# Attention and a two-layer FFN on one core: the 64 left-over keys of heads 8 to 19 join the softmax denominators on GpSimd instead of on TensorE

## The chip, the cores and the metric

The kernel runs on one core of a Trainium2 chip. The metric is the device time in microseconds (us) of one execution, as the median over several. TensorE (PE in the rows; PEld is its weight load), VectorE (DVE), ScalarE (ACT), GpSimd (POOL) and SyncE (SP) each work through a queue of their own in a fixed order; an instruction that has to wait holds up whatever stands behind it in its queue.

## The reference

Four sequences of 448 tokens, 12 heads of 64. Scores are capped by a tanh, softmax runs over the keys, and the heads' outputs, joined to rows of 768, pass through a layer norm without bias, two products with a ReLU between, and a residual:

```python
scores = cap * tanh((q @ k.T) / sqrt(64) / cap)
attn = exp(scores - max(scores)); attn = attn / (sum(attn) + 1e-9)
x = (attn @ v), heads joined                        # (4, 448, 768)
xn = (x - mean) / sqrt(var + 1e-6) * g_ln
out = x + relu(xn @ w_ch1) @ w_ch2                  # 768 -> 3072 -> 768
```

## The kernel before

Scores are kept with the keys on the partitions. 448 keys are three blocks of 128 and a rest of 64. Heads are worked on in quads (`quad`, line 499): four heads are two pairs, `p` = 0 and 1. For a pair, `products` (L707) makes the scores on TensorE (L724), ScalarE takes tanh (L769) and exp (L777) into a tile `es[p]` of 128 x (2 heads, 3 blocks, 448 queries); three such tiles exist at that stage. The rests of all four heads share one tile `er`: pair 0 on partitions 0 to 63, pair 1 on 64 to 127, each with its two heads side by side, 2 x 448 columns. Their scores are L750, their exp is L785.

Two things are made of the exponentials. The products with V go into two PSUM banks, by blocks (`pv`, L553) and then the rests (`pv_rest`, L560); they are copied out by L610 or L612. The denominators are sums over the keys: VectorE adds the three blocks of a pair into `s1` (L576, L578), two tiles of 128 x 896, of which two exist. Then `sums` (L630) multiplies `s1` with a column of ones on TensorE, one head to each 32 partitions of one PSUM bank: line L637, 4 products that show as 8 matmul records. What of the rests has to be added is done in one of two ways. For heads below `RESTS` = 20 the tile `er` is a second operand of `sums`: line L641, another 4 products with ones that are zero for the other pair's partitions. From head 20 on VectorE adds each half of `er` onto the same half of its pair's `s1` (L588, 64 x 896, one for each pair), and L641 is left out.

`finish` (L648) copies the sums to SBUF (`ss`; VectorE for heads 0 to 7, ScalarE from head 8), turns them on TensorE (L663) so that tokens lie on the partitions, adds epsilon and takes reciprocals on VectorE (L666, L669). The outputs are turned by four groups of two transposes (L677), each into a PSUM bank, and VectorE multiplies them by the reciprocals into the token tiles (L687). The padding of the turned tiles is zeroed on GpSimd (L620). After heads 8 to 11, the last of sequence 0, `norm` (L879) normalizes the first three token tiles: statistics (L859, L861), a power on GpSimd (L873), the subtraction and scaling on VectorE (L892), transposes (L900), and a split into two fp32r parts (L905 on ScalarE, L909 on VectorE). The first FFN products (L1020 to L1022) read these. FFN products then run in between the rest of the attention, up to 420 us; later stages are FFN alone (L1238 to L1241, L1331 to L1333).

GpSimd also unpacks the first four weight blocks (L949, L952, and their rounding in `round`, L493), which VectorE finishes (L955, L957, L496). The kernel's GpSimd DMAs (L1348) begin at 528 us.

No order is written out by hand. `add` (L158) records each operation with its engine, a cost, a due time, and the tiles it reads and writes. `emit` (L207) then plays the whole program through with those costs: each engine, when free, takes the operation of the earliest due time that is ready and whose buffers are to be had. The sequence that comes out is what each engine's queue gets. The waits on the chip come from the tiles that an instruction truly touches, not from `reads`. `LEAD` = 24 heads are due before the FFN's first products. The key `G` is GpSimd, `V` VectorE, `A` ScalarE, `T` TensorE.

Of the kernel before, what the change touches and what calls it, by code (L numbers as in the profile page):

```python
# [18 lines left out]
B, H, S, D = 4, 12, 448, 64  # L19
# [14 lines left out]
LEAD = 24  # L34
# [21 lines left out]
VEC2 = lambda n: 50 + 1.1 * n  # L56
# [28 lines left out]
GROUP = 4  # L85

FINE = 28
RESTS = 20
FIRST = 24


# [13 lines left out]
    e=('e', 3), e2=('e', 2), kh=('k', 2), kl=('k', 2), ot=('b', 4), ss=('b', 1), stage=('a', 3),  # L105
# [9 lines left out]
    e=('e', 2), t=('e', 2), ot=('b', 3), ss=('b', 1), stage=('a', 1),  # L115
# [32 lines left out]
class Order:  # L148
# [9 lines left out]
    def add(self, engines, fn, reads=(), writes=(), allocs=(), due=0.0, dma=0, after=(), lag=0.0):  # L158
        op = Op()
        (op.engine, op.cost), = engines.items()  # L160
        op.fn, op.due, op.dma, op.lag, op.seq = fn, due, dma, lag, len(self.ops)
        deps = set(after)
        for k in reads:
            deps.update(self.writer.get(k, ()))
        for k in writes:
            deps.update(self.writer.get(k, ()))
            deps.update(self.readers.get(k, ()))
        for k in writes:
            self.writer[k], self.readers[k] = [op], []
        for k in reads:  # L170
            self.readers.setdefault(k, []).append(op)
        deps.discard(op)
        op.left, op.outs, op.ready, op.end, op.wait, op.after = len(deps), [], 0.0, None, None, deps
        for d in deps:
            d.outs.append(op)
        bufs = {k[0] if isinstance(k, tuple) else k: 0 for k in (*reads, *writes, *allocs)}
        op.bufs = [b for b in bufs if isinstance(b, Buf)]
        for b in op.bufs:
            self.wide += b.wide and not b.users
            b.users += 1  # L180
            op.ready = max(op.ready, b.since)
        self.ops.append(op)
        return op
# [197 lines left out]
class Program:  # L381
# [25 lines left out]
    def buf(self, pool, tag, shape, dtype, bufs=1):  # L407
        size = 1
        for x in shape[1:]:
            size *= x  # L410
        kinds, tags = (GENERAL_KINDS, GENERAL_TAGS) if self.general else (KINDS, TAGS)
        if tag in tags:
            kind, n = tags[tag]
            self.limits[pool, tag] = n
            bufs, size = kinds[kind]
        else:
            kind = tag
        self.places[pool, kind] = bufs
        b = Buf(pool, kind, tag, shape, dtype)
        self.sizes[pool, kind] = max(size, self.sizes.get((pool, kind), 0))  # L420
        return b
# [77 lines left out]
    def quad(self, i, at):  # L499
# [3 lines left out]
        nc, add, buf = self.nc, self.add, self.buf  # L503
# [4 lines left out]
        for p in range(2):  # L508
            kq = self.given.get(i // 2 + p)
            if kq is None:  # L510
                kq = buf("att", "kq", [128, 2, S], F32)
                for k in range(2):
                    rows = slice(k * D, k * D + D)
                    add({"S": 550}, lambda e, h=i + 2 * p + k, rows=rows, kq=kq: nc.sync.dma_start(
                        out=kq.ap[rows], in_=self.kq[h, rows].rearrange("p (a s) -> p a s", a=2)),
                        writes=[(kq, k)], due=at(i + 2 * p) - PLAN["early"], dma=D * 2 * S * 4)
# [3 lines left out]
        for p in range(2):  # L520
            v = buf("att", "v", [128, 2, NJ, DV], F32)
            src = self.v[i + 2 * p:i + 2 * p + 2].rearrange("h p (j d) -> p h j d", d=DV)
            for a in range(2):
# [3 lines left out]
                    writes=[(v, a)], due=at(i + 2 * p) - PLAN["early"], dma=2 * KC * NJ * DV * 4)  # L527
# [8 lines left out]
        if split:  # L536
            parts.clear()
            for p, kq in enumerate(kqs):
                h, l = (buf("kr", t, [128, 2, S], F32R) for t in ("kh", "kl"))
                keys = [(kq, k) for k in range(2)]  # L540
                due = dues[p] - PLAN["qk"] - PLAN["ks"]
                add({"A": ACTS(2 * S)}, lambda e, h=h, kq=kq: self.round(e, h.ap, kq.ap), reads=keys, writes=[h], due=due)
                add({"V": VEC2(2 * S)}, lambda e, h=h, l=l, kq=kq: self.rest(e, l.ap, kq.ap, h.ap),
                    reads=[*keys, h], writes=[l], due=due)
# [20 lines left out]
        fine = i < FINE  # L565
# [6 lines left out]
        for p, e1 in enumerate(es):  # L572
            due = dues[p] - rush
            s1 = buf("att", "s1", [128, 2, S], F32)
            rows = slice(p * REST, p * REST + REST)
# [3 lines left out]
                out=s1.ap, in0=s1.ap, in1=e1.ap[:, :, 2], op=ALU.add), reads=[(e1, 0), (e1, 1)], writes=[s1], due=due)  # L579
            s1s.append(s1)  # L580

        if i < (FINE if self.general else RESTS):
            rests = [er]
        else:
            rests = []
            for p, s1 in enumerate(s1s):
                rows = slice(p * REST, p * REST + REST)
                add({"V": VEC2(2 * S)}, lambda e, s1=s1, rows=rows: nc.vector.tensor_tensor(  # L588
                    out=s1.ap[rows], in0=s1.ap[rows], in1=er.ap[rows], op=ALU.add), reads=[er], writes=[s1], due=dues[2] - rush)
        if merged:  # L590
            ps = self.sums(s1s, rests, dues[2] - rush, cost + F4(S), lambda: (pv(1), pv_rest()), [*v_all, *done(1), er], pos)
        else:
            for p in range(2):
                for blocks in [[j] for j in range(NK)] if i + p == 0 and not self.general else [range(NK)]:
                    add({"T": 200 + len(blocks) * F4(S)}, lambda e, p=p, blocks=blocks: pv(p, blocks),
                        reads=[*v_all, *(done(p) if len(blocks) > 1 else [(es[p], "e", j) for j in blocks])], writes=[pos[p]],
# [51 lines left out]
    def finish(self, i, pairs, ps, due, late):  # L648


        nc, add, buf = self.nc, self.add, self.buf
        b, h0 = divmod(i, H)
        part = HEADS[-(i < FRONT)]
        due += PLAN["fin"] if h0 + GROUP < H else 0
        ss, d0 = self.out_tile("ss", i, late)
        add({part["ss"]: dict(A=ACTP(S), V=VEC2(S))[part["ss"]]}, lambda e: self.copy(
            e, ss.ap[:, d0:d0 + S], ps.ap[:, :S]), reads=[ps], writes=[(ss, 0)], due=due)
        pr = buf("ps", "f", [128, 512], F32)
        r = buf("small", "r", [128, NK + 1, GROUP], F32, 2)

        def turn(e):
            for j in range(NK + 1):
                nc.tensor.transpose(pr.ap[:, j * 128:j * 128 + 128], ss.ap[:, j * 128:j * 128 + 128], self.ident)  # L663

        add({"T": 440}, turn, reads=[(ss, 0), (ss, 2)], writes=[pr], due=due)
        add({"V": 210}, lambda e: nc.vector.tensor_scalar(  # L666
            r.ap, pr.ap.rearrange("p (j c x) -> p j c x", j=NK + 1, c=GROUP)[:, :, :, 0], self.eps, None,
            op0=ALU.add), reads=[pr], writes=[r], due=due)
        add({"V": 220}, lambda e: nc.vector.reciprocal(r.ap, r.ap), writes=[r], due=due)  # L669
        W = GROUP * D  # L670
        cols = slice(h0 * D, h0 * D + W)
        for j, tl, p in self.token_tiles(b):
            pf = buf("ps", "f", [128, 512], F32)

            def turn(e, j=j, pf=pf):
                for c, ot in enumerate(pairs):
                    nc.tensor.transpose(pf.ap[:, c * 128:c * 128 + 128], ot.ap[:, j * 128:j * 128 + 128], self.ident)  # L677

            add({"T": len(pairs) * 110}, turn, reads=[(o, x) for o in pairs for x in (0, 2)] + [r] * self.general, writes=[pf], due=due)
            m = p.stop - p.start  # L680
            rows = lambda ap: ap.rearrange("p (h d) -> p h d", d=D)
            if tl < NA:
                writes, dst = [(self.home(tl)[0], tl, h0)], lambda tl=tl, p=p: self.x(tl)[p, cols]
            else:
                st = buf("att", "stage", [128, W], F32)
                writes, dst = [st], lambda st=st, p=p: st.ap[p]
            add({"V": VEC2(W)}, lambda e, j=j, p=p, m=m, dst=dst, pf=pf: nc.vector.tensor_tensor(  # L687
                out=rows(dst()), in0=rows(pf.ap[p, :W]), in1=r.ap[p, j].unsqueeze(2).to_broadcast([m, GROUP, D]),
                op=ALU.mult), reads=[pf, r], writes=writes, due=due)
            if tl >= NA:  # L690
                add({"V": 330}, lambda e, dst=dst, tl=tl, p=p: nc.vector.bn_stats(
                    self.stats.ap[p, tl % SLOTS, h0 // GROUP], dst()), reads=writes,
                    writes=[(self.stats, tl % SLOTS, h0 // GROUP, p.start)], due=due)
                add({"S": 550}, lambda e, dst=dst, tl=tl, p=p: nc.sync.dma_start(out=self.xd[tl][p, cols], in_=dst()),
                    reads=writes, writes=[("xd", tl, (h0, p.start))], due=due, dma=128 * W * 4)
# [883 lines left out]
```

## Time and profile before

| | us |
|---|---|
| median of 3 runs | 859.35 (858.87 to 860.08) |
| the profiled execution | 858.48 |
| its span, first to last instruction | 856.7 |
| mean granted TensorE clock | 0.999 |
| DMA traffic over the span | 148.96 MB, 174 GB/s |

The profile is of one execution. A share of busy time is an average over stages with different limits, so the rows below are read by stretch. A wait is put down to what released it. A matmul's duration is modelled, and neighbours overlap; what a group of matmuls costs is read from the start of the group to the start of the next.

### The profile page before, as it was taken

The page shows a single profiled execution, that of the slowest core. Times are in us where ns is not written, and L with a number is a line of the kernel's source. Part 1 is how long each engine was busy: PE and PEld are TensorE (multiplying, and loading weights), DVE is VectorE, ACT ScalarE, POOL GpSimd, SP SyncE. Part 2 cuts the span into 40 slices and gives each one's busy share as a digit, 9 for nine tenths or more (in the row PEclk, how much of TensorE's full clock was granted, in tenths as well). Part 3 has the DMA queues.
Part 4 walks back from the last instruction along what each step waited for, and adds up shares of the span by engine and source line. Part 5 has one row for each costly group of instructions (what it writes and reads, how often), then busy time and mean ns, then how long its engine had stood idle before and what let it go on. Part 6 is the DMA issues. An engine that isn't in the chain of part 4 may idle for free.

```text
span 856.7 us, 12856 instructions
## 1 busy us (share of the span) xinstructions
PE 845.3 (99%) x4700; PEld 705.2 (82%) x4700; DVE 702.6 (82%) x1157; ACT 512.1 (60%) x795; POOL 151.5 (18%) x198
## 2 busy tenths in 40 slices
PE   8999999999999999999999999999999999999997
PEld 4434477979879799799799989898988998999887
DVE  2689798878789788687689878888888888788896
ACT  7887777544653647354426646756575666566650
POOL 0233231101112111111110001223113211312210
PEclk9999999999999999999999999999999999999999
DMA  9696666565675774653673344897878888787984
GB/s 233 149 245 212 187 179 181 180 219 162 175 223 159 221 210 165 189 170 120 176 258 102 102 141 84 164 183 152 168 160 153 166 171 157 143 187 158 184 216 152
DMA packets 55579, 148.96 MB, mean 174 GB/s; under 512 B 7378, under 2 KB 20178, under 8 KB 55506
## 3 DMA queue, kind: packets, MB, share of 16 engines
q1 hardware_dynamic: 42256, 113.43, 44.9%
q0 software_dynamic: 12096, 33.04, 22.9%
q10 hardware_dynamic: 1154, 1.57, 0.5%
q8 instruction: 39, 0.64, 0.3%
q14 instruction: 34, 0.28, 0.1%
HBM read 87.46 MB, written 60.56 MB: 173 GB/s over the span
## 4 chain that ended last, share of the span: by engine, by line
PE 94%; ACT 2%; DVE 1%; issue 0%; POOL 0%; DVEq 0%; ACTq 0%
PE two L1238 7%; PE two L1241 7%; PE two L1239 7%; PE two L1331 7%; PE two L1333 7%; PE two L1332 7%; PE two L1020 6%; PE two L1049 6%; PE two L1022 6%; PE two L1021 6%; PE two L1051 6%; PE two L1050 6%; PE two L553 6%; PE two L724 5%; PE two L677 1%; PE two L637 1%
## 5 line engine op out<-in xcount | busy, mean ns | idle before, releaser
L1348 POOL DMA_DIRECT2D out_dram<-x x84 | 73.4, 1000 | 314.4 <-ACT x L1339 215.1
L1339 ACT ACTIVATE x<-two 128x384 f32<-128x384 f32 x168 | 79.6, 487 | 36.9 <-PE two L1333 26.2
L1020 PE MATMUL two<-hA,q 128*128 128x384 f32 x288 | 100.5, 349 | 0.0
L1238 PE MATMUL two<-X,q 128*128 128x512 f32 x252 | 99.2, 394 | 1.2 <-ACT y L1255 1.2
L1241 PE MATMUL two<-X,q 128*128 128x512 f32 x252 | 99.2, 394 | 0.0
L1239 PE MATMUL two<-X,q 128*128 128x512 f32 x252 | 99.0, 393 | 0.0
L1343 DVE TENSOR_TENSOR x<-two,x 128x384 f32<-128x384 f32 x144 | 77.0, 553 | 26.7 <-PE two L1333 22.8
L1049 PE MATMUL two<-w,hh 128*128 128x384 f32 x288 | 98.5, 342 | 0.0
L1022 PE MATMUL two<-hA,q 128*128 128x384 f32 x288 | 97.5, 339 | 0.0
L1021 PE MATMUL two<-lA,q 128*128 128x384 f32 x288 | 97.5, 338 | 0.0
L1051 PE MATMUL two<-w,hl 128*128 128x384 f32 x288 | 97.3, 338 | 0.0
L1050 PE MATMUL two<-w,hh 128*128 128x384 f32 x288 | 97.3, 338 | 0.0
L952 POOL TENSOR_SCALAR raw<-raw 128x768 f32<-128x768 f32 x48 | 48.7, 1017 | 229.4 <-ACT c L948 203.1
L1331 PE MATMUL two<-w,hop 128*128 128x384 f32 x264 | 89.0, 337 | 0.0
L1333 PE MATMUL two<-w,hop 128*128 128x384 f32 x264 | 88.8, 336 | 0.0
L1332 PE MATMUL two<-w,hop 128*128 128x384 f32 x264 | 88.8, 336 | 0.0
L1054 DVE TENSOR_TENSOR x<-two,x 128x384 f32<-128x384 f32 x144 | 76.0, 548 | 12.3 <-PE two L1051 11.8
L769 ACT ACTIVATE e<-two,sc 128x448 f32<-128x448 f32 (+1 forms) x108 | 75.0, 759 | 17.8 <-PE two L724 17.3
L489 ACT ACTIVATE w<-c 128x768 fp32r<-128x768 f32 x38 | 32.1, 846 | 60.6 <-DVE c L957 23.7
L1020 PEld LDWEIGHTS two<-hA,q 128*128 128x128 f32 x288 | 54.0, 188 | 10.9 <-issue 8.5
L777 ACT ACTIVATE e<-e,capt 128x1344 f32<-128x1344 f32 (+1 forms) x35 | 61.1, 1772 | 0.3
L553 PE MATMUL two<-e,v 128*64 128x448 f32 x288 | 59.2, 547 | 1.8 <-ACT e L769 0.9
(179 smaller groups left out, 1850.4 us busy)
## 6 DMA issues: line engine op xcount, KB each, us to landing
raw<-in_w_dram SPq DMA_DIRECT2D x48, 768.0 KB, 4.9
out_dram<-x POOLq DMA_DIRECT2D x84, 384.0 KB, 7.5
kept<-c SPq DMA_DIRECT2D x47, 384.0 KB, 5.5
d<-in_kq_dram SPq DMA_DIRECT2D x48, 224.0 KB, 5.6
d<-kept SPq DMA_DIRECT2D x23, 384.0 KB, 3.3
c<-kept SPq DMA_DIRECT2D x23, 384.0 KB, 7.9
v<-in_v_dram SPq DMA_DIRECT2D x24, 227.5 KB, 5.1
x<-out_dram SPq DMA_DIRECT2D x13, 384.0 KB, 5.4
```

What stands on the lines that cost most here:

```text
L1020: nc.tensor.matmul(ps.ap[:, :n], lhsT=w1h.ap[:, wc], rhs=xh.ap[:, c], start=(c == 0), stop=False)
L1021: nc.tensor.matmul(ps.ap[:, :n], lhsT=w1h.ap[:, wc], rhs=xl.ap[:, c], start=False, stop=False)
L1022: nc.tensor.matmul(ps.ap[:, :n], lhsT=w1l.ap[:, wc], rhs=xh.ap[:, c], start=False, stop=(c == CC - 1))
L1049: nc.tensor.matmul(o, lhsT=h[0].ap[:, mc], rhs=w[0].ap[:, hc], start=(f == 0), stop=False)
L1050: nc.tensor.matmul(o, lhsT=h[0].ap[:, mc], rhs=w[1].ap[:, hc], start=False, stop=False)
L1051: nc.tensor.matmul(o, lhsT=h[1].ap[:, mc], rhs=w[0].ap[:, hc], start=False, stop=(f == last))
L1238: nc.tensor.matmul(ps.ap, lhsT=wh.ap[:, wc], rhs=xs[c].ap[:, 0], start=start and c == 0, **o)
L1239: nc.tensor.matmul(ps.ap, lhsT=wh.ap[:, wc], rhs=xs[c].ap[:, 1], start=False, **o)
L1241: nc.tensor.matmul(ps.ap, lhsT=wl.ap[:, wc], rhs=xs[c].ap[:, 0], start=False, **o)
L1331: nc.tensor.matmul(o, lhsT=hh.ap[:, mc], rhs=wh.ap, start=begin, stop=False, **skip)
L1332: nc.tensor.matmul(o, lhsT=hh.ap[:, mc], rhs=wl.ap, start=False, stop=False, **skip)
L1333: nc.tensor.matmul(o, lhsT=hl.ap[:, mc], rhs=wh.ap, start=False, stop=True, **skip)
```

## The change

The number `RESTS` = 20 becomes a string with one letter for each of the first five quads: `T` for heads 0 to 7 (as before, L641), `G` for heads 8 to 19, and `V` (as before, L588) from head 20 on. For `G` the two additions of 64 x 896 that L588 does on VectorE are issued on GpSimd, and the planner counts 3000 ns for each; `sums` then has L637 alone. The additions read `er` and one `s1` each, and write that `s1`.

The second edit is in `finish`: for heads below `LEAD` = 24 the outputs' transposes (L677) name the copied sums `ss` among their reads. As they don't touch that tile, this holds for the planner's sequence and adds no semaphore.

```diff
--- before.py
+++ after.py
@@ -85,7 +85,7 @@
 GROUP = 4
 
 FINE = 28
-RESTS = 20
+RESTS = "TTGGG"
 FIRST = 24
 
 
@@ -579,13 +579,14 @@
                 out=s1.ap, in0=s1.ap, in1=e1.ap[:, :, 2], op=ALU.add), reads=[(e1, 0), (e1, 1)], writes=[s1], due=due)
             s1s.append(s1)
 
-        if i < (FINE if self.general else RESTS):
+        aside = RESTS[i // GROUP] if i < GROUP * len(RESTS) else "V"
+        if fine if self.general else aside == "T":
             rests = [er]
         else:
             rests = []
             for p, s1 in enumerate(s1s):
                 rows = slice(p * REST, p * REST + REST)
-                add({"V": VEC2(2 * S)}, lambda e, s1=s1, rows=rows: nc.vector.tensor_tensor(
+                add({"G": 3000} if aside == "G" else {"V": VEC2(2 * S)}, lambda e, s1=s1, rows=rows: self.eng(e).tensor_tensor(
                     out=s1.ap[rows], in0=s1.ap[rows], in1=er.ap[rows], op=ALU.add), reads=[er], writes=[s1], due=dues[2] - rush)
         if merged:
             ps = self.sums(s1s, rests, dues[2] - rush, cost + F4(S), lambda: (pv(1), pv_rest()), [*v_all, *done(1), er], pos)
@@ -676,7 +677,7 @@
                 for c, ot in enumerate(pairs):
                     nc.tensor.transpose(pf.ap[:, c * 128:c * 128 + 128], ot.ap[:, j * 128:j * 128 + 128], self.ident)
 
-            add({"T": len(pairs) * 110}, turn, reads=[(o, x) for o in pairs for x in (0, 2)] + [r] * self.general, writes=[pf], due=due)
+            add({"T": len(pairs) * 110}, turn, reads=[(o, x) for o in pairs for x in (0, 2)] + ([r] if self.general else [(ss, 0)] if i < LEAD else []), writes=[pf], due=due)
             m = p.stop - p.start
             rows = lambda ap: ap.rearrange("p (h d) -> p h d", d=D)
             if tl < NA:
```

## Rows read from the trace of the kernel before

**Rows 1.** The page: span; then busy us (share of the span) and instructions of each engine.

```profile
span 856.7 us, 12856 instructions
...
PE 845.3 (99%) x4700; PEld 705.2 (82%) x4700; DVE 702.6 (82%) x1157; ACT 512.1 (60%) x795; POOL 151.5 (18%) x198
```

**Rows 2.** Stretches: from:to, length, busy us (instructions) by engine, PE clock, DMA share, GB/s.

```profile
18.00:50.00 32.00, 31.89 (x196) 12.49 (x196) 24.07 (x38) 27.43 (x24) 6.18 (x11) 1.00 0.75 200
50.00:76.00 26.00, 25.04 (x149) 10.12 (x148) 21.34 (x37) 24.44 (x27) 12.24 (x13) 1.00 0.77 209
76.00:420.00 344.00, 344.00 (x2055) 281.40 (x2053) 284.35 (x436) 200.85 (x280) 54.67 (x72) 1.00 0.63 185
420.00:840.00 420.00, 418.82 (x2177) 382.28 (x2176) 358.68 (x617) 246.90 (x455) 76.93 (x87) 1.00 0.72 159
```

**Rows 3.** Waits of TensorE: waiter, releaser, us in total, times, longest.

```profile
PE two L900 <- DVE lA L909: 0.8, 1, 0.8
```

**Rows 4.** Chain of waits, 48 to 92 us: start us, us, what.

```profile
64.69 1.58 POOL mv L873
...
67.97 1.85 DVE xn L892 x3
...
74.78 1.07 PE two L900 x6
```

**Rows 5.** TensorE in order of time: start us, us, line, out<-in, count.

```profile
87.61 0.96 PE L637 MATMUL two<-d,ones 128*32 128x448 f32 x8
...
89.25 0.98 PE L560 MATMUL two<-d,v 64*64 64x448 f32 x8
...
105.12 0.96 PE L637 MATMUL two<-d,ones 128*32 128x448 f32 x8
106.01 0.98 PE L560 MATMUL two<-d,v 64*64 64x448 f32 x8
```

**Rows 6.** All matmuls of line L641: count, ns min/median/max, first and last start.

```profile
L641 PE MATMUL two<-d,ones x40: 539/539/539, 22.2 to 88.8; 128*32 128x448 f32 x40
```

**Rows 7.** ScalarE and VectorE in order of time: last inputs of the sums, heads 8 to 15.

```profile
46.33 1.04 ACT L785 ACTIVATE d<-d,capt 128x896 f32<-128x896 f32 x1
...
47.64 1.06 DVE L578 TENSOR_TENSOR d<-d,e 128x896 f32<-128x896 f32 x1
...
64.27 1.03 ACT L785 ACTIVATE d<-d,capt 128x896 f32<-128x896 f32 x1
...
66.97 1.08 DVE L578 TENSOR_TENSOR d<-d,e 128x896 f32<-128x896 f32 x1
```

**Rows 8.** GpSimd in order of time: start us, us, line, out<-in [idle before].

```profile
30.36 1.79 POOL L952 TENSOR_SCALAR raw<-raw 128x768 f32<-128x768 f32 x2
...
51.19 0.83 POOL L493 TENSOR_SCALAR q<-c 128x768 fp32r<-128x768 f32 x1 [5.43 <-DVE c L957]
...
101.05 1.63 POOL L952 TENSOR_SCALAR raw<-raw 128x768 f32<-128x768 f32 x1
```

**Rows 9.** VectorE in order of time: beside the first of rows 8, and after heads 16 to 19.

```profile
30.54 2.56 DVE L576 TENSOR_TENSOR d<-e 128x896 f32<-128x896 f32 x1 [0.17 <-ACT e L777]
...
91.48 1.09 DVE L576 TENSOR_TENSOR d<-e 128x896 f32<-128x896 f32 x1 [3.65 <-ACT e L777]
```

**Rows 10.** In order of time: TensorE and a ScalarE copy, heads 8 to 11; first FFN product.

```profile
50.17 0.96 PE L637 MATMUL two<-d,ones 128*32 128x448 f32 x8
...
52.76 0.66 PE L663 MATMUL two<-ident,b 128*128 128x128 f32 x4
...
56.36 0.96 ACT L610 ACTIVATE b<-two 128x448 f32<-128x448 f32 x2
...
57.89 1.09 PE L677 MATMUL two<-ident,b 128*128 128x128 f32 x8
...
84.65 0.44 PE L1020 MATMUL two<-hA,q 128*128 128x384 f32 x1
```

**Rows 11.** L576 over the whole run: count, ns min/median/max, first and last start.

```profile
L576 DVE TENSOR_TENSOR d<-e x24: 1029/1086/2555, 11.1 to 393.8; 128x896 f32<-128x896 f32 x24
```

## The prediction

> **What bounds the kernel now.** I began with the page's busy times: TensorE is busy 99% of the span, VectorE 82%, ScalarE 60%, GpSimd 18% [rows 1]. A busy matmul row is modelled, so I next took the stretches, to see where TensorE has any idle time that a rearranged queue could give back or add to. Between 18 and 50 us it lacks 0.11 us, between 50 and 76 us 0.96, between 76 and 420 us nothing, between 420 and 840 us 1.18 [rows 2]. So from 18 us on the span is a sum of TensorE's work with some 2.3 us of gaps in it, at the full granted clock, and work taken from TensorE should come off the end, unless a gap opens. Third, the list of TensorE's waits, for the largest gap near the change: 0.8 us, one wait of the layer norm's transposes L900 for VectorE's L909 [rows 3]. Fourth, the chain of waits around the edited quads. Between 52.9 and 74.8 us it does not run through TensorE for long: it goes over GpSimd's power L873, three subtractions L892 on VectorE, and ends at L900 [rows 4]. That is the one place before the FFN where VectorE and GpSimd decide when TensorE goes on, and the additions of heads 12 to 15 fall into it.
>
> **The products removed.** Duration alone misleads here, since the four 128x32 products of a group overlap: each record shows 539 ns [rows 6], which times eight would be 4.3 us. From start to start, heads 16 to 19 take 87.61 to 89.25 for L637 and L641 together, 1.64 us; heads 20 to 23, which have no L641, take 105.12 to 106.01, 0.89 us [rows 5]. The difference is 0.75 us. Of the 40 records 24 belong to the three quads (8 each) [rows 6], so TensorE loses 3 x 0.75 = 2.25 us of work. All three lie where TensorE is the busy engine; whether the two earlier ones also lie on the path is the question below.
>
> **The additions put on GpSimd.** Six of 64 x 896, each with two inputs in SBUF. The trace has no such instruction on GpSimd. From below: one input of 768 takes 0.83 us undisturbed [rows 8], for 896 columns that is 0.97. From above: L952 beside VectorE took 1.63 [rows 8]; for 896 columns and two inputs read one after the other, 2 x 1.63 x 896/768 = 3.8. I take 2.7: two undisturbed reads, 1.94, plus the 0.73 by which that L952 was longer than the 0.90 each of the undisturbed pair [rows 8]. It is a middle value, nearer to the undisturbed row because GpSimd is idle four fifths of the time. Two in turn are 5.4 us, and the planner counts 6.0, so the sums' products should be placed in TensorE's queue behind enough other work; the slack is 0.6 us with my value, 4.1 with the low end, and minus 1.6 with the high one.
>
> **What waits behind them.** The rests' exponentials end at 47.4 us for heads 8 to 11 and 65.3 for heads 12 to 15, the second pair's block sums at 48.7 and 68.0 [rows 7]. So the sums move 3 to 4 us back, from 50.2 [rows 10] to about 53.4 in the first case. In GpSimd's queue there stand then the rounding of a weight block, which ran at 51.19 [rows 8], memsets, unpacking, and the power of the layer norm at 64.69 [rows 4]. The weights' first use is at 84.65 us [rows 10], so a delay of 2 to 3 us has cover. The power has none: an addition ahead of it would push the chain back by a whole addition. By the due times it should stand ahead, since it is due with heads 8 to 11. GpSimd issues no DMA at this stage; SyncE's loads of keys wait for buffers only. The two `s1` tiles are held some 3 to 4 us longer. If the next quad's L576 has to wait for one, the three exponential tiles come free later; at heads 16 to 19 there is cover, since VectorE idles 3.65 us before the next L576 at 91.48 [rows 9].
>
> **The transposes that wait.** In the queue of before, the denominators' transposes already precede the outputs', 52.76 before 57.89 for heads 8 to 11, and the outputs' had to wait for ScalarE's copies at 56.4 anyway [rows 10]. The later sums thus hide behind that copy; what they add on the way to the norm is at most the sums' own copy and L663 behind it, 0.5 + 0.6 = 1.1 us [rows 10]. I count nothing, as long as TensorE has scores of the next quad to do; bounds 0 and 1.1, and no gain, because the edit only delays.
>
> **VectorE beside GpSimd.** This is the cost that the planner's numbers don't hold. While GpSimd ran two L952 in 1.79 us, an L576 took 2.56 us [rows 8, 9] where its median is 1.09 [rows 11]: 1.47 us lost, 82% of GpSimd's time. The SBUF page of the Trainium skill ("SBUF — State Buffer", section "Who interferes with whom") has this as a rule: an instruction of VectorE with two SBUF inputs and one of GpSimd that reads SBUF exclude each other. The rows agree: of the 1.61 us that the two shared, VectorE lost 1.47 [rows 8, 9]. For heads 12 to 15, the additions fall between 65.3 and 71.5 us, and VectorE has L578, L892 and the weights there, on the chain [rows 4, 7]. Two undisturbed additions, 3.9 us, would take up to 82% of that from it, 3.2 us. For heads 16 to 19 the idle 3.65 us covers the same loss, and for heads 8 to 11 VectorE works ahead of what TensorE needs.
>
> **The sum.** TensorE's work minus 2.25 us. New gaps: I take 0.25 us out of 0 to 3.2, near the low end, because TensorE has hardly any gap elsewhere before the FFN [rows 2] and the queue is laid out anew with the later sums known. Against the profiled execution: 858.48 - 2.25 + 0.25 = 856.48. That execution is 0.87 us below the median of the runs, so 857.35 in the terms of the median.
>
> **The rivals.** First, the earlier savings are swallowed: TensorE reaches L900 sooner and waits there longer, because VectorE's chain is what ends last at 74.78 [rows 4]. For it speaks that the wait is there already [rows 3]; against it, that in the 26 us around it TensorE found other work but for 0.96 us [rows 2]. Then only heads 16 to 19 pay: 859.35 - 0.75 = 858.6. Second, VectorE is set back: the full 3.2 us appear as a gap before L900 and nothing fills it: 859.35 - 2.25 + 3.2 = 860.3. It decides once GpSimd's additions stand between the power and L892. Third, the slower end: the additions take longer than the planner's 3.0 us, and the sums' products, in TensorE's fixed queue, wait. With 3.8 us each they are 1.6 us late, in three quads 4.8: 859.35 - 2.25 + 4.8 = 861.9. It decides from 3.0 us for one addition on; for it speaks the contention of [rows 8], against it that the first of a pair can start before the second pair's block sums are done [rows 7]. Fourth, better: the new queue also loses the 0.96 us of gaps before 76 us: 859.35 - 2.25 - 0.96 = 856.1. That the change doesn't take L641 away at all I give no chance: the planner's operation for `sums` simply has no rests.
>
> **How the numbers follow.** Forecast 0.38, swallowed 0.20, VectorE set back 0.20, sums late 0.10, better 0.12. A measurement of this kernel can tell about 0.2% from no change, 1.72 us: faster is below 857.63, slower above 861.07. The forecast and the better case are faster, 0.50 together; the forecast lies only 0.28 us inside that bound. Swallowed and set back are within it, 0.40; sums late is slower, 0.10. The range takes in the better case with half a microsecond for gaps elsewhere in the new queue (the 1.18 us after 420 us can go either way), and the set-back case with the 1.1 us of the sums' copy partly on top: 855.6 to 861.2. It leaves out the slow end.
>
> **What would show it.** In the profile after: L641 with 16 matmul records instead of 40; six additions of 64 x 896 on GpSimd, below 3.0 us each; no wait of L637 for GpSimd above 0.3 us; 2.2 us less TensorE work before the first FFN product; TensorE's gaps between 50 and 76 us at 0.7 to 1.5 us, and the ones after 420 us near 1.2. A wait of L637 for GpSimd would prove the third rival, a longer wait of L900 the first or second (the second if VectorE's instructions beside the additions show 2 us and more). I am wrong in the other direction if the gaps vanish. Should the work before the FFN shrink by 2.25 us and the end not move, some later stage took it back, which nothing in these rows leads me to expect.

## The result, and the profile after

The changed kernel takes 865.2 us against 859.14 in the same session; the ratio is 1.0063, with an interval of 1.0052 to 1.0074. It is 0.63% slower, where 0.23% faster was forecast. One of the changed kernel's six executions took 2125.8 us; the ratio leaves it out, and the median of the other five is 864.94. The profiled execution took 864.05 us, its span is 862.1: 5.6 and 5.4 us above the one of before.

In the lines of all kernels from here on, what stood below L581 stands one line lower (L892 is L893, L952 is L953); the additions on GpSimd are L589. First the page's busy times of after, which answer to [rows 1], and the busy times by stretch (the columns after the stretch's length are TensorE, its weight loads, VectorE, ScalarE and GpSimd, then the granted clock):

```profile
PE 843.1 (98%) x4676; PEld 703.5 (82%) x4676; DVE 712.1 (83%) x1157; ACT 512.1 (59%) x795; POOL 167.8 (19%) x204
```

```profile
18.00:50.00 32.00, 31.63 (x196) 12.50 (x196) 23.55 (x38) 27.44 (x24) 9.09 (x12) 1.00 0.70 190
50.00:76.00 26.00, 22.01 (x129) 7.72 (x125) 23.25 (x30) 23.11 (x23) 18.23 (x16) 1.00 0.83 239
76.00:107.00 31.00, 28.49 (x169) 12.14 (x170) 27.84 (x45) 25.28 (x31) 8.62 (x11) 1.00 0.69 200
107.00:176.00 69.00, 67.74 (x406) 56.82 (x405) 63.33 (x101) 43.61 (x63) 17.26 (x21) 1.00 0.55 163
176.00:420.00 244.00, 244.00 (x1456) 210.75 (x1455) 198.00 (x294) 131.83 (x189) 35.12 (x42) 1.00 0.62 182
420.00:840.00 420.00, 418.82 (x2175) 380.67 (x2174) 358.64 (x615) 248.58 (x458) 77.98 (x88) 1.00 0.73 161
```

The removed products are gone: 24 matmul records fewer, 2.25 us of work. But TensorE's idle time (length minus busy) is now 0.37 us up to 50 us, 3.99 up to 76, 2.51 up to 107, 1.26 up to 176, nothing up to 420 and 1.18 after. That is 9.3 us against 2.25 in [rows 2], 7.1 more, and 7.1 - 2.25 = 4.8 of the span's 5.4. All of it is made before 176 us; the last 0.6 us lies at the two ends, where TensorE idles 0.4 us less before 18 us and 0.95 more behind 840. VectorE is 9.5 us busier with the same 1157 instructions (702.6 in [rows 1]).

The list of TensorE's waits from 18 to 176 us in after, the longest first (waiter, what it waited for, total, times, longest):

```profile
PE two L901 <- DVE xn L893: 2.4, 3, 1.3
PE two L678 <- DVE r L667: 1.3, 1, 1.3
PE two L901 <- DVE lA L910: 1.3, 1, 1.3
PE two L725 <- DVE lA L910: 0.9, 1, 0.9
```

Before had one wait for VectorE here, of 0.8 us [rows 3]. The four longest of after all name VectorE; the shorter ones behind them, 0.9 us and less, are three for ScalarE, which e1 below has too, and one more for VectorE. This is what VectorE and GpSimd did meanwhile, from the timeline of after (start, duration, engine, line; "x2" is two instructions in a row; in brackets the idle time before and what ended it):

```profile
49.57 2.17 DVE L496 TENSOR_TENSOR q<-c,q 128x768 fp32r<-128x768 f32 x1
51.66 2.83 DVE L958 SCALAR_TENSOR_TENSOR c<-c,raw 128x768 int32<-128x768 int32 x1
55.53 1.67 DVE L496 TENSOR_TENSOR q<-c,q 128x768 fp32r<-128x768 f32 x1 [1.03 <-POOL q L493]
65.98 2.83 DVE L578 TENSOR_TENSOR d<-d,e 128x896 f32<-128x896 f32 x1
70.74 1.95 DVE L868 TENSOR_TENSOR mv<-mv 128x3 f32<-128x3 f32 x1
73.74 2.91 DVE L893 TENSOR_SCALAR xn<-x,mv 128x768 f32<-128x768 f32 x3
```

```profile
47.73 5.95 POOL L589 TENSOR_TENSOR d<-d,d 64x896 f32<-64x896 f32 x2 [1.71 <-DVE d L576]
54.66 0.84 POOL L493 TENSOR_SCALAR q<-c 128x768 fp32r<-128x768 f32 x1 [0.98 <-DVE c L958]
64.93 2.93 POOL L589 TENSOR_TENSOR d<-d,d 64x896 f32<-64x896 f32 x1
68.97 1.53 POOL L874 TENSOR_TENSOR mv<-mv,mhalf 128x3 f32<-128x3 f32 x1 [1.11 <-DVE mv L872]
70.58 2.09 POOL L589 TENSOR_TENSOR d<-d,d 64x896 f32<-64x896 f32 x1
```

An undisturbed addition takes 2.09 us. Beside it VectorE does not go slower, it stands still: L868 works on 128 x 3 elements, otherwise a matter of 0.17 us, started at 70.74 and ended at 72.69, when the addition ended at 72.67. The subtraction L893 began at 73.74 instead of 67.97, behind the instructions that were held. That it took 2.91 us for three (1.85 in [rows 4]) is not the additions' doing: none ran beside it, and in e1 below, with short additions, it took 2.45. From 49 to 58 us the chain of waits of after runs through VectorE's held instructions and GpSimd's unpacking instead of through TensorE (start, duration, what):

```profile
49.64 2.09 DVE q L496
51.74 2.77 DVE c L958
...
54.66 0.84 POOL q L493
55.49 0.90 POOL c L950
56.47 1.50 POOL raw L953
```

So two suspects work together: VectorE held up while an addition runs, and GpSimd's queue, in which the weights' rounding and unpacking stand behind the additions, with VectorE's queue waiting for them. In after the first of the two ends last: the additions were over at 53.68, and L493 then waited 0.98 us more for the held L958.

### The profile page after: what moved, and what is told of

Its sections match the earlier page's. It is cut to its first block, busy times and chain, and to the rows that moved or that the text cites. A ratio compares the mean times of both kernels' runs of the same rounds, so it can differ in the third digit from the quotient of the medians.

```text
span 862.1 us, 12819 instructions
## 1 busy us (share of the span) xinstructions
PE 843.1 (98%) x4676; PEld 703.5 (82%) x4676; DVE 712.1 (83%) x1157; ACT 512.1 (59%) x795; POOL 167.8 (19%) x204
## 4 chain that ended last, share of the span: by engine, by line
PE 90%; DVE 5%; ACT 2%; DMA 1%; issue 0%; POOL 0%; SPq 0%; DVEq 0%; ACTq 0%; POOLq 0%
PE two L1239 7%; PE two L1242 7%; PE two L1240 7%; PE two L1332 7%; PE two L1334 7%; PE two L1333 7%; PE two L1021 6%; PE two L1050 6%; PE two L1052 6%; PE two L1051 6%; PE two L1023 6%; PE two L1022 6%; PE two L553 5%; PE two L725 4%; PE two L560 1%; ACT e L770 1%
## 5 line engine op out<-in xcount | busy, mean ns | idle before, releaser
L953 POOL TENSOR_SCALAR raw<-raw 128x768 f32<-128x768 f32 x48 | 52.1, 1087 | 235.3 <-ACT c L949 200.7
```

## The experiments

**The same queues, with short additions.** The first pair asks whether the additions' length costs the time, or the newly laid sequence. e1 has the changed kernel's sequence on every engine.

```diff
-                    out=s1.ap[rows], in0=s1.ap[rows], in1=er.ap[rows], op=ALU.add), reads=[er], writes=[s1], due=dues[2] - rush)
+                    out=s1.ap[rows, :, :4 if aside == "G" else S], in0=s1.ap[rows, :, :4 if aside == "G" else S],
+                    in1=er.ap[rows, :, :4 if aside == "G" else S], op=ALU.add), reads=[er], writes=[s1], due=dues[2] - rush)
```

> The changed kernel with the very same queue on every engine, but each GpSimd addition covers 4 of the 448 columns of each head (8 instead of 896 elements on 64 partitions); the other columns of the rests are missing from the denominators. This leaves out GpSimd's time and its collisions with VectorE and keeps everything else, the later place of the sums among it. Theory A (the additions block VectorE on the chip): most of the 6 us go, 857.0 to 858.5, the stretched VectorE instructions (L868 1.95 us, L578 2.83, L958 2.83) fall back to 0.2, 1.1 and 1.0. Rival B (the newly laid out queues, with later sums, are worse by themselves): 862 to 865, and the waits of L901 stay above 2 us.

Measured: 858.06 us against 858.72, ratio 0.9991 (0.9982 to 1.0). In e2 the additions are left out altogether:

```diff
-RESTS = "TTGGG"
+RESTS = "TTNNN"
-            for p, s1 in enumerate(s1s):
+            for p, s1 in enumerate(s1s if aside != "N" else []):
```

> The changed kernel without any addition of the rests for heads 8 to 19, neither on TensorE nor on GpSimd; the denominators of these heads lack the rests. It shows what taking L641 away is worth where nothing replaces it. If TensorE's work is on the path in all three quads: 2.25 us below before, 856.9. If the two earlier savings are swallowed before the layer norm: 858.4. If a newly laid out queue costs by itself: 859 and above.

Measured: 858.01 against 858.72, 0.9989 (0.998 to 0.9998). Two things follow. The length of six GpSimd additions, with all queues kept, is worth 0.0072 of 859, 6 to 7 us. And the work that the change takes from TensorE is worth 0.7 us even at no price: idle time between 18 and 176 us is 3.0 us in e1 where before has 1.1 [rows 2].

**The two edits apart.** e3 keeps the second edit alone (`RESTS = "TTTTT"`), e4 the first alone (without `ss` among the reads of L677).

> The second edit alone: all five quads keep their products with ones (L641), the outputs' transposes wait for the sums' copy in the planner. Theory A: no change, 859.1 within 0.7 us. Rival C (the second edit costs TensorE gaps, such as the 1.3 us before the last outputs' transposes of heads 8 to 11): 860.0 to 861.5.

> The first edit alone: GpSimd's additions, but the outputs' transposes don't wait for the sums' copy in the planner. Theory A: about as slow as the whole change, 863 to 866. Rival C: faster than the whole change by the gaps that the second edit makes, 860 to 862.

Measured: e3 859.12 against 858.72, 1.0004 (0.9995 to 1.0013), no difference. e4 867.13, 1.0098 (1.0082 to 1.0113), above both of its ranges. By itself the second edit does nothing. With the additions on GpSimd the kernel without it is about 0.0035 of 859, 3 us, slower still. In e4's profile that is not a longer wait: over the span TensorE idles 17.5 us there and 19.0 in after, but it is 3.4 us busier at a mean granted clock of 0.995. So it is not shown that the edit as such saves the 3 us.

**Which quads.** e5, e6 and e7 put one quad each on GpSimd, e8 the three on VectorE. For e5 (e6 has "TTTGT", e7 "TTTTG", e8 "TTVVV"):

```diff
-RESTS = "TTGGG"
+RESTS = "TTGTT"
```

> GpSimd's additions for heads 8 to 11 alone; heads 12 to 19 keep their products with ones. If the loss comes from collisions on VectorE's way to the first layer norm, part of it is here: the two additions hold up the weights' unpacking (L496 2.17, L958 2.83 us in the whole change) and set the outputs back, 859.5 to 862. If only heads 12 to 15 matter: 858.4 to 859.1.

> GpSimd's additions for heads 12 to 15 alone. Theory A: these stand beside the layer norm (power behind an addition, L868, L578 and L893 held up) and carry most of the loss, 861 to 864, with waits of L901 for L893 of 2 us and more. If the loss is spread evenly over the six additions (about 2.2 us for each quad, less 0.2 saved): 861.0; if it needs the delays of heads 8 to 11 before it: 858.5 to 860.

> GpSimd's additions for heads 16 to 19 alone, where VectorE idled 3.65 us in the kernel before. Theory A: no collision that matters, 0.2 to 0.75 us saved, 858.0 to 858.6. If every collision costs wherever it lies: 860 to 861.

> The additions of heads 8 to 19 on VectorE itself, as from head 20 on: six times 1.09 us more there, 6.5 us, with no GpSimd beside them, and the planner knows of them. Theory A (being held up by GpSimd costs VectorE more, 9.5 us of busy time in the whole change, and at places that the planner does not know): faster than the whole change, 859 to 862. If VectorE's sheer load before the layer norm is what decides, whoever causes it: 863 to 866.

Measured against 858.95: 863.78, 1.0052 (1.004 to 1.0064); 864.92, 1.0073 (1.0061 to 1.0085); 861.09, 1.0026 (1.0017 to 1.0035); and e8 860.89, 1.0023 (1.0014 to 1.0033). e5 and e6 came out above all that was expected for them. Heads 12 to 15 alone cost as much as all three quads, so these effects don't add up. And VectorE doing the additions itself costs less than GpSimd doing them: its busy time is 710.4 us in e8, below the 712.1 of after.

Each of these kernels has a sequence of its own, however. So e9, e10 and e11 repeat e7, e6 and e5 with the short additions of e1, each with its twin's sequence.

> The queues of e7 (additions for heads 16 to 19 alone), instruction for instruction, but GpSimd adds only 4 of the 448 columns of each head, so most of these heads' rests are left out of the sums and GpSimd is busy for well under a microsecond. If e7's loss of 2.1 us comes from the additions running beside VectorE, it goes: 858 to 859 us, and TensorE's idle time between 76 and 107 us (1.59 in e7) falls to that of the kernel without additions (0.6 to 0.9). If it comes from the newly laid queues, it stays: 860.5 to 861.5 us with the idle time of e7. For e7 the second is the likelier: VectorE's busy time was hardly longer there.

> The queues of e6 (heads 12 to 15 alone) with 4 of 448 columns added on GpSimd; the rest of these heads' rests is left out. If the additions running beside VectorE cost e6's 6.0 us: 858 to 859.5 us, and the idle time of TensorE between 50 and 76 us (2.83 in e6) goes to about 1. If the laid queues with 83 switches between attention and FFN products cost it: 863 us or more. Expected is the first, with at most 1 us left.

> The queues of e5 (heads 8 to 11 alone) with 4 of 448 columns added on GpSimd; the rest of these heads' rests is left out. If the additions running beside VectorE cost e5's 4.8 us: 858 to 859.5 us, idle time of TensorE between 50 and 76 us down from 2.45 to about 1, and a granted clock at the higher level between 78 and 86 us. If the laid queues cost it: 862 us or more, with the lower clock in the same place. Expected is the first.

Measured against 858.99: 860.76, 1.0019 (1.0011 to 1.0028); 861.5, 1.0026 (1.0017 to 1.0035); 860.71, 1.0025 (1.0016 to 1.0034). Where "858 to 859.5" was expected for e10 and e11 that was a miss. The sequences alone cost 0.2 to 0.3%; the additions' length costs another 0.3 to 0.5% in e5 and e6, and in e7 nothing that can be told. A sequence laid anew is thus a throw of its own: minus 0.1% in e1, plus 0.2 to 0.3% here. What in these sequences costs it I did not settle.

**A planner that knows.** e12 counts 2150 ns for an addition and holds VectorE as taken until it ends.

```diff
+                if e == "G" and cost == 2150:
+                    free["V"] = max(free["V"], o.end)
-                add({"G": 3000} if aside == "G" else {"V": VEC2(2 * S)}, lambda e, s1=s1, rows=rows: self.eng(e).tensor_tensor(
+                add({"G": 2150} if aside == "G" else {"V": VEC2(2 * S)}, lambda e, s1=s1, rows=rows: self.eng(e).tensor_tensor(
```

> All six additions in full on GpSimd, as in the changed kernel; only the planner differs: it counts 2150 ns for one, about what was measured, and holds VectorE as taken until the addition ends. If the loss comes from a sequence that was laid without knowing that VectorE is held up, a sequence that knows it wins back most: 859 to 861.5 us. If VectorE's time itself is what is missing before 176 us (some 9.5 us more busy), no sequence helps: 863 us or more. Expected is about 862, between the two, since VectorE's added time stays and only its place changes.

Measured: 865.77 against 858.99, 1.0066 (1.0051 to 1.0081). Nothing comes back in the time, and "about 862" was a miss. In the profile TensorE idles 0.8 us less over the span than in after, and is 3.3 us busier at a mean granted clock of 0.995. This one sequence doesn't show that no sequence could.

**By which way the length costs.** The next four keep the changed kernel's sequence. e13 adds 4 columns for the sums, and behind that a full 64 x 896 on the side (a tile that is zeroed once before), for which no one waits. e14 has three `memset(aux, 0.0)` in that place, e15 two `tensor_scalar(aux, aux, 1.0, None, op0=ALU.mult)`; e16 cuts the true additions in four of 224 columns. The added line of e13:

```diff
+                        nc.gpsimd.tensor_tensor(out=aux, in0=aux, in1=aux, op=ALU.add)
```

> The queues of the changed kernel. GpSimd adds only 4 of the 448 columns of each head to the sums (the rest is left out), and right behind each of these short additions it does a full one, 64 x 896, on a part of a token tile that is not in use yet, so no other engine waits for its end. If VectorE is held up by the addition as such: as slow as the changed kernel, 863.5 to 866 us, with VectorE's instructions beside the additions stretched by 1 to 2 us. If the loss came from the sums or the tiles' release waiting for the additions' ends: 858 to 859.5 us. Expected is the first.

> The queues of the changed kernel, 4 of 448 columns added as in e13, and behind each short addition three fills of 64 x 896 with zero on GpSimd, together as long as an addition or a little longer, which read nothing. If the loss came from GpSimd's queue being late for the layer norm's power and the unpacking behind the additions: 862 us or more. If it came from a collision on the operands that both engines read: 858 to 859.5 us, and no stretched instruction on VectorE. Expected is the second.

> As e14, but behind each short addition two multiplications of 64 x 896 by a number, which read one operand each and together take about as long as an addition. If any reading by GpSimd holds VectorE up: 862.5 us or more, with stretched instructions. If only an instruction with two operands from SBUF does: 858 to 859.5 us. The second is the likelier: the unpacking in the kernel before also reads one operand, and VectorE's instructions beside it were not stretched to more than 1.85 us.

> The changed kernel with nothing left out, each addition cut into four of 64 x 224. If an instruction of VectorE is held until the instruction of GpSimd ends, a hold is at most about 0.6 us instead of 2.1, and much comes back: 860 to 863 us. If VectorE is held for the whole of GpSimd's work in any case, or slowed in proportion: 864 to 867 us, since the work is as long or longer. Expected is the second with some 6 in 10.

Measured against 858.88: e13 861.87, 1.0034 (1.0021 to 1.0047); e14 860.56, 1.002 (1.0011 to 1.0029); e15 874.3, 1.018 (1.0167 to 1.0193); e16 862.83, 1.0054 (1.0039 to 1.0069). Both e13 and e14 came out between their two alternatives. The side additions of e13 are shorter than the true ones, 1.67 us for most, and TensorE's list of waits does not name GpSimd; so 0.43% over e1 comes without sums that wait. The fills, which read nothing, cost 0.3% over e1. In e14's timeline VectorE's instruction beside them is not stretched (0.93), but the next weight block is late, since GpSimd gets to it at 54.84; VectorE first, then GpSimd:

```profile
49.85 0.93 DVE L503 TENSOR_TENSOR q<-c,q 128x768 fp32r<-128x768 f32 x1
55.71 1.67 DVE L503 TENSOR_TENSOR q<-c,q 128x768 fp32r<-128x768 f32 x1 [4.06 <-POOL q L500]
49.27 2.63 POOL L603 MEMSET x<- 64x896 f32 x3
52.11 2.64 POOL L603 MEMSET x<- 64x896 f32 x3
54.84 0.84 POOL L500 TENSOR_SCALAR q<-c 128x768 fp32r<-128x768 f32 x1
```

(L503 and L500 are L496 and L493 of after.) So the queue alone is a price. The SBUF page of the Trainium skill ("SBUF — State Buffer", section "Who interferes with whom") says that a VectorE instruction with two SBUF inputs collides with GpSimd instructions that read SBUF, not with those that only write, and it calls the ports that the two share an exclusive lock: the 0.93 us beside the fills and L868's end 0.02 us behind the addition's agree.

In its time e15 is no fair test of one operand against two: a multiplication of 64 x 896 took 2.5 us, so GpSimd was held 5 us each time, and VectorE also had to wait 5.2 us once for the side tile. What it does show is the queue's price when it grows, in VectorE's waits from 40 to 107 us:

```profile
DVE q L503 <- POOL q L500: 8.7, 1, 8.7
DVE x L702 <- POOL x L603: 5.2, 1, 5.2
DVE raw L970 <- POOL raw L967: 3.7, 3, 2.1
```

Its trace does answer the question for these multiplications; GpSimd and what VectorE did beside it:

```profile
48.59 4.99 POOL L603 TENSOR_SCALAR x<-x 64x896 f32<-64x896 f32 x2
49.15 1.19 DVE L503 TENSOR_TENSOR q<-c,q 128x768 fp32r<-128x768 f32 x1
50.25 0.95 DVE L972 SCALAR_TENSOR_TENSOR c<-c,raw 128x768 int32<-128x768 int32 x1
```

L972 has two operands in SBUF and took the 0.95 us of e1, L503 0.25 more than its 0.94. Beside the later multiplications VectorE lost at most 0.7 us at a time; it was never held to their end. They read SBUF, so here the measurement goes against the page's exclusive lock; why is open. Other instructions of GpSimd with one operand do hold VectorE: beside the unpacking L950 the second L496 of after took 1.67 us, and the L576 of [rows 9] took 2.56, more than the 1.85 that the expectation of e15 names as the most.

e16 came out at the less expected of its two ends, though not clearly below after, whose 1.0063 lies within its interval: the first two additions took 8.00 us instead of 5.95, since VectorE gets in between the pieces; VectorE's busy time fell to 708.1, but the second L496 started at 56.10 instead of 55.53, and the sums waited for GpSimd once, 1.0 us. One price was exchanged for the other.

**Where the time is made.** The last pair keeps the sequence too, with full additions for heads 8 to 11 alone (e17) and for heads 12 to 19 alone (e18). Against e1, for e17 (e18 has `i == 2 * GROUP`, and the line of `in1` goes the same way):

```diff
-                    out=s1.ap[rows, :, :4 if aside == "G" else S], in0=s1.ap[rows, :, :4 if aside == "G" else S],
+                    out=s1.ap[rows, :, :4 if aside == "G" and i != 2 * GROUP else S], in0=s1.ap[rows, :, :4 if aside == "G" and i != 2 * GROUP else S],
```

> The queues of the changed kernel; the two additions of heads 8 to 11 are full, the four of heads 12 to 19 add only 4 of 448 columns of each head (the rest is left out). If the two additions in a row make GpSimd's rounding of a weight block late and VectorE's queue with it: VectorE's second weight instruction L496 starts at about 55.5 us instead of 52.2, VectorE is 3 to 4 us late from there to 110 us, and the time is 861 to 862.5 us. If heads 8 to 11 have cover, as the prediction had it: 858 to 859 us. Expected is the first.

> The queues of the changed kernel; the four additions of heads 12 to 19 are full, the two of heads 8 to 11 add only 4 of 448 columns of each head (the rest is left out). If the stretched instructions of VectorE around the layer norm are a cost of their own: L496 at about 52.2 us, VectorE 2.5 to 4 us late by 110 us, and the time 860.5 to 862.5 us. If only the late rounding counted: 858 to 859 us. Expected is the first, and that the two shares, each above the 858.06 of e1, add up to the 7 us within about 1.5 us.

Measured against 858.53: e17 859.83, 1.002 (1.0009 to 1.0031); e18 862.35, 1.0041 (1.0028 to 1.0054). e17 was expected at 861 or more: its second L496 came at 55.39 as expected, 3.2 us behind e1's 52.23, but by 68 us VectorE had made up a third. Above e1 the two are worth 0.29 and 0.50%, together 0.79 where after has 0.72: on one and the same sequence the shares do add up. TensorE's waits between 50 and 76 us show the two places, first the largest of e17, then that of e18 (their lines stand one lower still):

```profile
PE two L679 <- DVE r L668: 1.4, 1, 1.4
PE two L902 <- DVE xn L894: 2.1, 3, 1.0
```

After has both, 1.3 and 1.3 in that window.

**One number behind all of them.** In these kernels VectorE's queue is the same, instruction for instruction. So one instruction, a second block sum L578 at 110 us in e1, dates how late VectorE is once the additions are over; its rows in e1, e14 (where it is L585) and after:

```profile
110.32 1.08 DVE L578 TENSOR_TENSOR d<-d,e 128x896 f32<-128x896 f32 x1
```

```profile
113.62 1.08 DVE L585 TENSOR_TENSOR d<-d,e 128x896 f32<-128x896 f32 x1
```

```profile
116.23 1.08 DVE L578 TENSOR_TENSOR d<-d,e 128x896 f32<-128x896 f32 x1
```

| kernel | that L578 starts, us | behind e1, us | the same in % of 859 | time above e1, % of before |
|---|---|---|---|---|
| e1 short additions | 110.32 | 0 | 0 | 0 |
| e17 full for heads 8 to 11 | 112.05 | 1.73 | 0.20 | 0.29 |
| e14 fills | 113.62 | 3.30 | 0.38 | 0.29 |
| e13 additions on the side | 114.41 | 4.09 | 0.48 | 0.43 |
| e18 full for heads 12 to 19 | 115.38 | 5.06 | 0.59 | 0.50 |
| e16 cut in four | 115.40 | 5.08 | 0.59 | 0.63 |
| after | 116.23 | 5.91 | 0.69 | 0.72 |
| e15 multiplications on the side | 126.15 | 15.83 | 1.84 | 1.89 |

The last two columns agree within 0.1%, about the half width of the intervals. The kernel's end moves as much as VectorE is late when the additions are over, by whichever of the two ways it became late.

## Why the prediction was wrong, step by step

**The work removed** was right: 24 of 40 records gone, and the queues work as described.

**The additions' length** was nearly right: 2.7 us forecast, 2.62 mean measured (5.95 for the first two together, then 2.93, 2.09, 2.09 and 2.76). The sign "below 3.0 us each" failed for one, the first, with 3.19. The third rival, sums late, was to decide from 3.0 us on and did not come: TensorE's list has no wait for GpSimd. Only the weight loads of L638 waited, 0.7 and 0.3 us, while matmuls ran.

**What waits behind them** failed. "A delay of 2 to 3 us has cover" was read from TensorE's first use of the weights, 84.65 us in [rows 10]. The one that waits is not TensorE but VectorE, whose L496 takes up the block that L493 rounds, and behind L496 stand the next quad's block sums. Before, that L493 ran at 51.19 [rows 8]; after, at 54.66. In e1, with the same queues, L496 started at 52.23, in after at 55.53, in e14 at 55.71. In after that L493 waited for VectorE's L958, which the second addition held up, in e14 for the fills ahead of it. The power did not stand ahead of the additions as it "should": the first one of heads 12 to 15 ran before it, from 64.93 to 67.86. What it waited for was VectorE (1.11 us idle ahead of L874), where L872 stood behind the L578 that this addition held up; so it ran at 68.97 instead of 64.69.

**VectorE beside GpSimd** was the right mechanism, and the price for the one place that was charged was about right; what failed is the rest of the list. The same three L576 on VectorE, first in e1, then in after, show how late VectorE is ahead of the additions of heads 12 to 15, behind them, and behind those of heads 16 to 19:

```profile
62.48 1.07 DVE L576 TENSOR_TENSOR d<-e 128x896 f32<-128x896 f32 x1
71.90 1.08 DVE L576 TENSOR_TENSOR d<-e 128x896 f32<-128x896 f32 x1
89.29 1.09 DVE L576 TENSOR_TENSOR d<-e 128x896 f32<-128x896 f32 x1 [1.52 <-ACT e L779]
```

```profile
64.53 1.39 DVE L576 TENSOR_TENSOR d<-e 128x896 f32<-128x896 f32 x1
77.44 1.08 DVE L576 TENSOR_TENSOR d<-e 128x896 f32<-128x896 f32 x1
95.20 1.09 DVE L576 TENSOR_TENSOR d<-e 128x896 f32<-128x896 f32 x1 [0.67 <-ACT e L778]
```

It is 2.05, 5.54 and 5.91 us late. Heads 12 to 15 thus cost 3.5 us (3.2 in e18), where up to 3.2 was charged, though the sum then took hardly any of it. "VectorE works ahead of what TensorE needs" for heads 8 to 11 failed: they cost 1.9 us (0.2 of the 2.05 was there before them) and had been put at nothing. For heads 16 to 19 the idle time did cover most of the loss in after: 0.4 us is left, since the idle time ahead of the last L576 fell from 1.52 to 0.67 us; in e18 1.6 us is left. In VectorE's busy time the additions cost 712.1 - 704.0 = 8.1 us over e1. "VectorE set back" was the right rival for one place, without the two others. The sum goes: VectorE 5.9 us late at 110 us, where 3.2 was the most I allowed.

**The new gaps** were the term of the sum that broke: 0.25 us taken, 7.1 measured. One part of it has nothing to do with collisions. With short additions (e1) or none (e2), new gaps took 2.0 and 0.8 us, and 0.7 us was left of the 2.25; why e2 gained no more with the smaller gaps is open. The other 5.1 us of after came with the additions' length. The rival "swallowed" had the size of the first part, 0.75 us left, but by luck: it put the loss at L900, between 50 and 76 us, and there e1 idles 0.7 us where before has 0.96; its new gaps lie behind that, 0.85 us up to 107 and 1.26 up to 176. The reason given against both rivals, that TensorE "found other work but for 0.96 us" between 50 and 76 us, described the old sequence at its old VectorE times. It said nothing of what TensorE would find once VectorE is late.

**The transposes that wait** cost nothing by themselves (e3), as counted. That the kernel would be slower still without it (e4) was not foreseen; the lower clock of e4's profile accounts for it, and what brings that about is open.

**The range** ended at 861.2. Its upper end was the price of one disturbed place; there was a second one at heads 8 to 11 and a rest at heads 16 to 19, their delays add up along VectorE's queue, and the new sequence has gaps of its own.

## What to carry to other kernels

An engine that is 18% busy is not free: an instruction moved onto it can hold up another engine, as six additions held up VectorE here for 8.1 us, and delays whatever stands behind it in its queue, and whoever waits in order for that. Follow each queue past the moved instruction to the next engine that waits, not to the final user. To price such a move, keep the sequence and change only the length of the instruction; a kernel with another sequence differs by some 0.2 to 0.3% for that alone, and can't be used to split a loss of 0.6%.

## What the runs showed of the hardware beside that

In some executions the granted clock was lower for a few us. In e5's profile it was 0.54 from 78 to 82 us and 0.61 from 82 to 86, of the two levels, 1.2 and 2.4 GHz, mostly the lower. TensorE had stood idle before that for 2.0 of the 4 us from 56 on and for 1.6 of the 4 from 74 on. Such gaps alone don't decide it: in the profile of after it idled 1.8 and 2.1 us in these two stretches, and the clock stayed at 1.00. The same twelve products of that place, in e5 and in after (start, duration):

```profile
82.38 3.83 PE L553 MATMUL two<-e,v 128*64 128x448 f32 x12
```

```profile
82.11 2.48 PE L553 MATMUL two<-e,v 128*64 128x448 f32 x12
```

A busy share doesn't show this, since the slower products count as busy: TensorE is busy 4.00 us of 4 from 82 on in both. Among the executions of after 862.76 us came at a mean clock of 1.000, 864.05 at 0.999, and 864.94, 865.46 and 865.58 at 0.996 or 0.997. So up to some 3 us of a single execution go with the clock; that the gaps bring the lower clock about is not shown.

A multiplication of 64 x 896 by a number took 2.5 us on GpSimd (L603 in e15, 4.99 for two), more than the addition of two such operands (2.09, or 1.67 in e13 with one and the same operand), and far more than the unpacking's 0.9 for 128 x 768 [rows 8]. Why was not tried.
